# Folded products in 64-column halves, paired short pieces in the transforms, folds partly on VectorE, and all gates in the first stage: a gated mix of a spectral filter and a mixture of single-row experts

## The chip, the cores and the metric

The kernel runs on one core of a Trainium2 chip. The metric is the device time of one execution in microseconds (us). TensorE (PE, with its weight loads PEld), VectorE (DVE), ScalarE (ACT), GpSimd (POOL) and SyncE (SP) each run their own instructions in order; a queue issues its DMAs in order, and 16 DMA engines carry them.

## The reference

The input x has 2048 tokens of 576 numbers. One branch filters x in the spectrum, the other picks for each token and each of 32 heads one of 4096 experts by a product key (the best of 64 keys on the first half of a query, the best of 64 on the second), and a gate mixes the two.

```python
X = rfft2(x); y_a = irfft2(X * (w_r + 1j * w_i), (S, D))       # S=2048, D=576
q = einsum("nd,dhc->nhc", x, w_q); q1, q2 = q[..., :128], q[..., 128:]
s1 = einsum("nhd,ed->nhe", q1, k1); s2 = einsum("nhd,ed->nhe", q2, k2)
e = argmax(s1) * 64 + argmax(s2)                               # K = 1, so softmax is 1
y_b = einsum("nhk,nhkd->nd", gelu(einsum("nd,nhkd->nhk", x, u[e])), v[e])
g = sigmoid((x * gate_w).sum(-1)); out = g * y_a + (1 - g) * y_b
```

Rows of u and v lie side by side in memory, so that one gathered row is 4608 bytes. 2048 x 32 of them are 302 MB.

## The kernel before

The tokens make 16 tiles t of 128. The work has two stages that use the same memory after one another.

**Score stage.** Keys are folded into the query weights ahead of the scores: for each chunk c of four heads and each of five slices i of the model width, `build_m` multiplies the transposed query weights (tile `wq`, loaded by SP into the ring `uv`, L351) with the keys (`kT`): 8 matmuls of 128 columns each, of which 64 are used. ACT and one more pair of matmuls split the product into a high and a low part, `mh` and `ml`; there are 40 such builds. 64 steps (c, tp), one for each chunk and pair of tiles, then form the scores: 28 matmuls of 128x512 into one PSUM buffer `p`. DVE takes the maxima (`mx`, L463), ACT marks where the score equals its maximum (`sg`, L471, L482), DVE turns the marks of two steps into an index (`sq`, L488 to L499, `fe`, L502), and ACT writes it (`ei`, L504). Each tile's x is transposed on PE and split into `xh`, `xo`, `xq` (`split_x`).

From an index on, POOL gathers (L537; 512 gathers of 576 KB, four to a group) into the ring `uv` of 12 buffers, with 2 more (`uv2`) in the second stage. A group of one tile and one chunk is then: four dot products on DVE (L548), gelu on ACT (L554), weights on DVE (L561), and the sum over v either on DVE (L574) or by ACT (L586) and transposing matmuls on PE, with the total added from PSUM at L624 (`yt`). Tiles 0 to 9 (`E_T`) are gathered while scores are still formed, tiles 10 to 15 (`L_SEQ`, the late tiles) behind them.

**Transform stage.** When the memory of the score stage comes free, SP loads `kr` (L713), the late tiles' x (`xl`, L392), the matrix `fi` (L717), the gate's weights `gr` (L718), the filter `w` (L762) and twiddles `tw` (L755, then three copies on ACT, L756 to L758). 16 `fold`s multiply sums and differences of the two halves of a tile's columns with `kr`; ten units (`f2`, `f4`, `f5` on DVE at L781 to L784, `f6`) make the transform, the product with the filter and the way back; `invert` makes the output of each tile, and `mix` adds the branches. Between the folds and the units stand no barriers: gathers and sums of the late tiles go on beside them.

The order on each engine is set ahead by a planner (class `Plan`): a list scheduler that has a due time for each job (`when(s) = 16 + s * TPS` for step s, offsets `AT_*`, `AHEAD`, `TLAG`), a duration for each operation, delays between engines (`HOPS`) and for a gather (`LEAD`, `LAND`). Its result is the program; on the chip each engine follows it and waits where it must. It also decides which slot of a ring a buffer gets.

The gates: for tiles 0 to 9 the product x * gate_w and its sum are formed early (L399, with the weights in a `uv` buffer). For tiles 10 to 15 they are formed at the change of the stages (L403, `close_gates`) from `xl` and `gr`, followed by the sigmoid.

```python
plan("POOL", ISSUE, at - ahead, go, [(g, 0), (g, 1)], [("ei", t // 2, c)], move=MOVE, after=gate_by)
for n, t in enumerate(range(NT)):
    fold(t, T0 + AT_FOLD + FPACE * 1.3 * n)
```

## Time and profile before

| | us |
|---|---|
| runs, median of 3 | 963.69 (962.10 to 973.03) |
| profiled execution, its own time | 963.87 |
| its span | 962.1 |
| PE busy in the span | 912.2 (95%) |
| PEld / DVE / ACT / POOL busy | 770.5 / 827.3 / 649.7 / 576.5 |
| bytes moved by DMA | 344.17 MB, mean 358 GB/s |

The profile is one execution: a page of sums, and views that are asked of its trace. In a timeline row stand the start, the time from the first start to the last end, the engine, the line of the program, the operation with its output and inputs, the count, and in brackets the idle time before it and what ended it. A view of windows gives the busy time of each engine in stretches of the span, with the granted TensorE clock (PEclk) and the share of the DMA engines that was busy. A view of waits sums the idle time of an engine by what ended it. One fp32 matmul leaves two records of each kind, a PE record and a PEld record (the 640 records `p<-kT,uv` belong to the 320 matmuls of the 40 builds). A busy PE is not PE at its peak, since a matmul's end is modelled.

### The profile page before, as it was taken

Reading aid. Unit: us, or ns where it says so; the run is one execution under the profiler, and the core shown is the slowest. Engines: PE = TensorE matmul, PEld = TensorE weight load, DVE = VectorE, ACT = ScalarE, POOL = GpSimd, SP = SyncE. Lnnn points to the kernel's source line nnn. Section 1 sums busy time; section 2 is a strip of 40 time slices with the busy share of each in tenths; the row PEclk is TensorE's granted clock in tenths of the full one; section 3 lists DMA queues with packets and bytes.
Section 4 is the critical chain, followed back from the end, with each engine's and each line's share of the span. In section 5 each row is a group of like instructions: output and inputs, shape, how many; then the busy total and the mean of one; then the engine's idle time right before and its main releaser. Section 6 shows DMA issues by size and latency. Waiting matters only on the chain.

```text
span 962.1 us, 16497 instructions
## 1 busy us (share of the span) xinstructions
PE 912.2 (95%) x5192; PEld 770.5 (80%) x5192; DVE 827.3 (86%) x2019; ACT 649.7 (68%) x1970; POOL 576.5 (60%) x516
## 2 busy tenths in 40 slices
PE   7999999999999999999999996899999999999996
PEld 7888888878778878878778784678888888888875
DVE  1898889998999999998999997776788888868877
ACT  3697887787787788787788686344556566575444
POOL 0236546756756757757757666256766666677662
PEclk9999999999999999999999999899999999999999
DMA  9469969999999999999999999778999999999997
GB/s 340 155 242 339 386 255 358 387 357 359 367 356 339 396 343 372 383 347 366 374 350 339 355 368 406 296 284 328 409 410 410 409 409 406 408 404 413 413 415 254
DMA packets 89803, 344.17 MB, mean 358 GB/s; under 512 B 10098, under 2 KB 10612, under 8 KB 89716
## 3 DMA queue, kind: packets, MB, share of 16 engines
q0 software_dynamic: 73728, 302.02, 81.9%
q1 hardware_dynamic: 15988, 41.09, 11.3%
q8 instruction: 42, 0.69, 0.3%
q14 instruction: 45, 0.37, 0.1%
HBM read 338.35 MB, written 4.72 MB: 357 GB/s over the span
## 4 chain that ended last, share of the span: by engine, by line
PE 46%; DVE 24%; DMA 15%; ACT 7%; issue 6%; POOL 2%; DVEq 0%; SPq 0%; POOLq 0%; ACTq 0%
PE p L307 46%; DMA uv<-uv,ei 12%; DVE uv L548 8%; DVE xn L574 7%; ACT sg L471 3%; DVE mx L463 3%; ACT uv L586 3%; DMA gr<-gw 2%; POOL uv L537 2%; DVE sq L488 1%; DVE yt L624 1%; DMA kr<-t_kr 1%; DVE bt L848 0%; DVE sq L495 0%; DVE sq L496 0%
## 5 line engine op out<-in xcount | busy, mean ns | idle before, releaser
L537 POOL DMA_INDIRECT uv<-uv,ei x512 | 576.3, 1126 | 373.3 <-PE p L307 116.2
L471 ACT ACTIVATE sg<-p,mx 128x64 bf16<-128x64 f32 x1024 | 227.5, 361 | 53.0 <-DVE mx L463 46.0
L548 DVE SCALAR_TENSOR_TENSOR uv<-uv,xn 128x576 f32<-128x576 f32 x320 | 236.9, 753 | 19.3 <-DMA uv<-uv,ei 12.0
L307 PE MATMUL p<-mh,xh 128*128 128x512 f32 x512 | 204.3, 399 | 10.7 <-ACT sg L471 10.0
L574 DVE SCALAR_TENSOR_TENSOR xn<-uv,a,xn 128x576 f32<-128x576 f32 x248 | 201.7, 815 | 1.2
L586 ACT ACTIVATE uv<-uv,a 128x576 f32<-128x576 f32 x256 | 178.2, 768 | 35.0 <-DVE a L561 32.9
L307 PE MATMUL p<-ml,xh 128*128 128x512 f32 x512 | 200.5, 392 | 0.0
L307 PE MATMUL p<-mh,xo 128*128 128x512 f32 x512 | 200.2, 391 | 0.0
L548 DVE SCALAR_TENSOR_TENSOR uv<-uv,xl 128x576 f32<-128x576 f32 x192 | 142.1, 756 | 34.0 <-DMA uv<-uv,ei 32.8
L307 PE MATMUL p<-ident,uv 128*128 128x128 f32 x1310 | 161.5, 275 | 10.0 <-ACT uv L586 9.9
L307 PEld LDWEIGHTS p<-ident,uv 128*128 128x128 f32 x1310 | 144.9, 141 | 27.2 <-ACT uv L586 16.8
L307 PEld LDWEIGHTS p<-mh,xh 128*128 128x128 f32 x512 | 96.5, 188 | 29.6 <-ACT sg L471 11.2
L307 PEld LDWEIGHTS p<-mh,xo 128*128 128x128 f32 x512 | 96.5, 188 | 20.7
L307 PEld LDWEIGHTS p<-ml,xh 128*128 128x128 f32 x512 | 96.7, 189 | 17.4
L554 ACT ACTIVATE b<-z 128x4 f32<-128x4 f32 (+1 forms) x131 | 27.5, 210 | 113.4 <-DVE uv L548 112.6
L307 PE MATMUL p<-fi,bt 128*128 128x289 f32 x384 | 99.3, 410 | 0.1
L307 PEld LDWEIGHTS p<-fi,bt 128*128 128x128 f32 x384 | 83.1, 243 | 10.6 <-PE p L307 0.6
L463 DVE TENSOR_REDUCE mx<-p 128x16 f32<-128x1024 f32 x64 | 78.1, 1220 | 9.2 <-PE p L307 9.2
L307 PEld LDWEIGHTS p<-kT,uv 128*128 128x128 f32 x640 | 76.4, 194 | 2.5 <-PE p L307 0.5
L307 PE MATMUL p<-kT,uv 128*128 128x128 f32 x640 | 77.8, 277 | 0.4 <-PE p L307 0.3
L482 ACT ACTIVATE sg<-sg 128x256 bf16<-128x256 bf16 x192 | 71.8, 442 | 0.9
L307 PE MATMUL p<-mh,xq 128*128 128x512 f32 x128 | 50.1, 392 | 0.0
(107 smaller groups left out, 936.7 us busy)
## 6 DMA issues: line engine op xcount, KB each, us to landing
uv<-wqT SPq DMA_DIRECT2D x40, 512.0 KB, 6.7
uv<-uv,ei POOLq DMA_INDIRECT x512, 7.4
w<-wri SPq DMA_DIRECT2D x16, 289.0 KB, 6.7
out<-xn SPq DMA_DIRECT2D x13, 288.0 KB, 6.4
xn<-xn SPq DMA_DIRECT2D x10, 288.0 KB, 6.9
tw<-t_tw SPq DMA_DIRECT2D x9, 256.0 KB, 6.3
uv<-xn SPq DMA_DIRECT2D x6, 288.0 KB, 7.2
xl<-xn SPq DMA_DIRECT2D x6, 288.0 KB, 12.6
```

What stands on the lines that cost most here:

```text
L307: after("PE", nc.tensor.matmul(*args, **kw))
L463: dv(dve(1024), at, lambda: nc.vector.tensor_reduce(mv.ap[:, 2 * tp : 2 * tp + 2, :], ps.ap.rearrange("p a (g e) -> p a g e", e=E), AX.X, ...
L471: on("ACT", actv(sg.ap[:, j, g, :], ps.ap[:, j, g * E : g * E + E], AF.Sign, bias=mv.ap[:, 2 * tp + j, g : g + 1], scale=-1.0))
L482: ac(0.307, at, lambda b=b: actv(s2()[:, :, b * Q : b * Q + Q], s2()[:, :, b * Q : b * Q + Q], AF.Copy, bias=b / 4), [sg], [])
L488: dv(0.336, at, lambda: vt(sq.ap[:, k], s2()[:, :, : E // 2], s2()[:, :, E // 2 :], ALU.min), [(sq, k)], [sg])
L537: on("POOL", nc.gpsimd.indirect_dma_start(out=g.ap.rearrange("p a d -> p (a d)"), out_offset=None, in_=uv, in_offset=bass.IndirectOffsetOn ...
L548: dv(0.677, at, lambda k=k, g=rows[k]: stt(g.ap[:, 0, :], g.ap[:, 0, :], 1.0, x.ap, op0=ALU.mult, op1=ALU.mult, accum_out=z.ap[:, k : k + 1]),
L554: ac(0.1, at + AT_GELU, lambda k0=k0, k1=k1: actv(b.ap[:, k0:k1], z.ap[:, k0:k1], AF.Gelu_apprx_tanh), [(b, k0)], [(z, k) for k in ks], ta ...
L574: dv(0.731, at, lambda v=v, s=s: stt(y.ap, v(), s(), y.ap, op0=ALU.mult, op1=ALU.add), [y], [(rows[k], 1), (a, k)])
L586: ac(0.667, at + AT_SCALE, lambda k=k, v=v: actv(v(), v(), AF.Copy, scale=a.ap[:, k : k + 1]), [(rows[k], 1)], [(a, k)])
L624: dv(dve(n), at, lambda: vt(to(), of(), to(), ALU.add), [y], [pd])
```

## The change

Nothing of the mathematics changes. Six things do.

- `build_m`: 16 matmuls of 64 weight columns by 64 moving columns take the place of 8 of 128 by 128. They alternate between the upper and lower 64 output partitions; no unused column is formed.
- `fold`: for the 12 tiles of `FOLD_V`, DVE forms the sum and the difference of the two halves (two operations of 128x288), ACT copies 32 columns, and 6 matmuls follow: 4 of 128 columns and 2 of 64. For the other 4 tiles the same 12 matmuls stay, with equal widths next to each other.
- `f2` and `invert`: the third piece of a sum, two matmuls over 128 rows half of which met zeros, becomes two matmuls over 64 rows each (`tails`), next to each other. `f2` takes the two members of a pair in one go.
- All 16 gates are formed in the first stage, from x as `split_x` loaded it, late tiles first; `gr`, its load and the six products of L403 are gone. The sigmoid follows at once.
- The fifth transpose of `split_x` is 128 wide, as the others are.
- The planner: other delays, loads timed apart from gathers, a pace of 8.37 in place of 8.45, other due times (`AHEAD`, `TLAG`, `AT_*`), other steps for the builds, other pairs of late tiles. Lines of the program shift by about 10 (L351 becomes L357, L471 L482, L537 L548 and so on).

```diff
-                if got.move:
-                    dma = max(dma, t + (LEAD if eng == "POOL" else 1.96)) + got.move
-                    got.end = dma + (LAND if eng == "POOL" else 1.1)
+                if got.move and eng == "POOL":
+                    dma = max(dma, t + LEAD) + got.move
+                    got.end = dma + LAND
+                elif got.move:
+                    a = max(loads, t + 1.96)
+                    loads = a + got.move * (SLOW if dma > a else 1.0)
+                    dma = max(dma, a) + got.move
...
-            w = P if i < ND - 1 else D - 4 * P
-            mm(flat[:w, i * P : i * P + P], v[:, i * P : i * P + w], ident, is_transpose=True, skip_group_check=True, start=True, stop=True)
+            lo = min(i * P, D - P)
+            mm(flat[:, i * P : i * P + P], v[:, lo : lo + P], ident, is_transpose=True, skip_group_check=True, start=True, stop=True)
...
-    def gates(t, w, at, junk=None):
-        x = xs[t]
+    natural = {}
+
+    def gates(t, w, at):
+        x, v = natural[t]
         two = lambda a: a.rearrange("p (r d) -> p r d", r=2)
-        if junk is None:
-            out_ = lambda: two(w.ap[:, 1, :])
-            dv(dve(576), at, lambda: stt(
-                out_(), two(x.ap), 1.0, two(w.ap[:, 0, :]), op0=ALU.mult, op1=ALU.mult, accum_out=gz[:, t : t + 1]),
-                [("gz", t), (w, 1)], [x, (w, 0)])
-        else:
-            dv(dve(576), at, lambda: stt(
-                junk.ap[:, :, :288], two(x.ap), 1.0, two(w.ap), op0=ALU.mult, op1=ALU.mult, accum_out=gz[:, t : t + 1]),
-                [("gz", t), junk], [x, w])
+        dv(dve(576), at, lambda: stt(
+            two(w.ap[:, 1, :]), two(v()), 1.0, two(w.ap[:, 0, :]), op0=ALU.mult, op1=ALU.mult, accum_out=gz[:, t : t + 1]),
+            [("gz", t), (w, 1)], [x, (w, 0)])
+
+    def close_gates(at):
+        allz = [("gz", t) for t in range(NT)]
+        ac(0.2, at, lambda: actv(ge, gz, AF.Exp, scale=-1.0), ["ge"], allz, table="exp")
+        dv(0.1, at, lambda: nc.vector.tensor_scalar(ge, ge, 1.0, None, op0=ALU.add), ["ge"], [])
+        dv(0.2, at, lambda: nc.vector.reciprocal(gate, ge), ["gate"], ["ge"])
+        dv(0.1, at, lambda: nc.vector.tensor_scalar(gone, gate, -1.0, 1.0, op0=ALU.mult, op1=ALU.add), ["gone"], ["gate"])
+        dv(0.1, at, lambda: nc.vector.tensor_scalar(gsc, gate, 2.0 / (S * D), None, op0=ALU.mult), ["gsc"], ["gate"])
...
-                half = g % 2
-                mm(
-                    pv()[:, g, :], wq.ap[:, g, :],
-                    kTb.ap[:, half * 64 : half * 64 + 128], start=g % 4 == 0, stop=True, skip_group_check=True)
-
-        plan("PE", 8 * BUILT, at, go, [pm], [wq, kTb], after=after)
+                k = kTb.ap[:, g % 2 * E : g % 2 * E + E]
+                for m in (0, E):
+                    mm(pv()[m : m + E, g, :E], wq.ap[:, g, m : m + E], k, start=g % 4 == 0, stop=True, skip_group_check=True)
+
+        plan("PE", 8 * BUILT + 0.2, at, go, [pm], [wq, kTb], after=after)
...
-    for t in E_T:
-        gates(t, gw1, when(0) + GATE * t)
+    for n, t in enumerate(L_SEQ + E_T):
+        gates(t, gw1, when(0) + GATE0 + GATE * n)
+    close_gates(when(0) + GATE0 + GATE * NT)
...
-    ld(0.5, T0 + 15, lambda: nc.sync.dma_start(gw2.ap, gw.partition_broadcast(P)), [gw2])
...
+        if t in FOLD_V:
+            eo = buf("f5", [P, 640])
+            o, e, r = (eo, 0), (eo, 1), (eo, 2)
+            dv(dve(288), at, lambda: vt(eo.ap[:, 288:576], x.ap[:, :288], x.ap[:, 288:], ALU.add), [e], [x])
+            ac(0.12, at, lambda: actv(eo.ap[:, 576:608], x.ap[:, 288:320], AF.Copy), [r], [x])
+            dv(dve(288), at, lambda: vt(eo.ap[:, :288], x.ap[:, :288], x.ap[:, 288:], ALU.subtract), [o], [x])
+
+            def go():
+                pf = pb.ap.rearrange("p a b -> p (a b)")
+                for i, m0, lo, w in ((0, 0, 288, P), (1, 0, 416, P), (3, 0, 0, P), (4, 0, P, P), (2, 0, 544, E), (2, E, 256, E)):
+                    mm(pf[m0 : m0 + w, i * P : (i + 1) * P], eo.ap[:, lo : lo + w], kr.ap[:, 0, :], start=i in (0, 4), stop=True, skip_group_check=True)
+
+            plan("PE", 1.3, at, go, [pb], [o, e, r, (kr, 0)])
+            evacuate(t, pb, at)
+            return
 
         def go():
             pf = pb.ap.rearrange("p a b -> p (a b)")
-            for i, m0, lo, w, n, sign in ((0, 0, 0, P, P, 0), (1, 0, P, P, P, 0), (2, 0, 2 * P, E, 32, 0), (2, E, 2 * P, E, 32, 1), (3, 0, 0, P, P, 1), (4, 0, P, P, P, 1)):
-                for k, (at_, m) in enumerate(((lo, w), (DF - 1 + lo, n))):
-                    mm(pf[m0 : m0 + m, i * P : (i + 1) * P], x.ap[:, at_ : at_ + m], kr.ap[:, sign * k, :],
-                       start=i in (0, 4) and not k, stop=k == 1, skip_group_check=True)
-
-        plan("PE", 12 * 0.213, at, go, [pb], [x, (kr, 0), (kr, 1)])
+            hi = DF - 1
+            for i, m0, w, at_, sign, first, last in (
+                    (0, 0, P, 0, 0, 1, 0), (0, 0, P, hi, 0, 0, 1), (1, 0, P, P, 0, 0, 0), (1, 0, P, hi + P, 0, 0, 1),
+                    (3, 0, P, 0, 0, 0, 0), (3, 0, P, hi, 1, 0, 1), (4, 0, P, P, 0, 1, 0), (4, 0, P, hi + P, 1, 0, 1),
+                    (2, 0, E, 2 * P, 0, 0, 0), (2, E, E, 2 * P, 0, 0, 0), (2, 0, 32, hi + 2 * P, 0, 0, 1), (2, E, 32, hi + 2 * P, 1, 0, 1)):
+                mm(pf[m0 : m0 + w, i * P : (i + 1) * P], x.ap[:, at_ : at_ + w], kr.ap[:, sign, :],
+                   start=bool(first), stop=bool(last), skip_group_check=True)
+
+        plan("PE", 2.5, at, go, [pb], [x, (kr, 0), (kr, 1)])
+        evacuate(t, pb, at)
...
+    def tails(parts):
+        for o, b in parts:
+            for r in range(2):
+                for i in (3 * r, 3 * r + 1):
+                    mm(o(r), b(i), fi.ap[:, i, :], start=i == 3 * r, stop=False)
+        for o, b in parts:
+            for r in range(2):
+                mm(o(r), b(2)[r * E : r * E + E], fi.ap[r * E : r * E + E, 2 + 3 * r, :], start=False, stop=True)
+
+    def f2(qs, at):
+        ps = [psum() for _ in qs]
 
         def go():
-            for r in range(2):
-                for n, i in enumerate(((0, 1, 2), (3, 4, 2))[r]):
-                    mm(p.ap[:, r, :DF], BT.ap[:, i, :, q], fi.ap[:, 3 * r + n, :], start=n == 0, stop=n == 2)
-
-        plan("PE", 6 * pe(DF), at, go, [p], [fi, (fi, "ends"), (BT, "q", q)] + [(BT, "in", t, i) for t in range(NT) for i in range(2)])
-        return p
+            tails([(lambda r, p=p: p.ap[:, r, :DF], lambda i, q=q: BT.ap[:, i, :, q]) for p, q in zip(ps, qs)])
+
+        plan("PE", 5 * len(qs) * pe(DF) + 0.2, at, go, ps, [fi, (fi, "ends")] + [(BT, "q", q) for q in qs] + [(BT, "in", t, i) for t in range(NT) for i in range(2)])
+        return ps
...
+        pair = f2((k2,) if k2 in (0, 8) else (k2, 8 + k2), at)
+        pc = pair[0]
...
-    def close_gates(at):
-        jg = psum()
-        for t in L_SEQ:
-            gates(t, gw2, at, jg)
...
-            for r in range(2):
-                for m, i in enumerate((3 * r, 3 * r + 1, 2)):
-                    mm(p.ap[:, r, :DF], BT.ap[:, i, t * 8 : t * 8 + 8, :].rearrange("p j q -> p (j q)"),
-                       fi.ap[:, 3 * r + m, :], start=m == 0, stop=m == 2)
-
-        plan("PE", 6 * pe(DF), at, go, [p], [fi, (fi, "ends")] + every)
+            tails([(lambda r: p.ap[:, r, :DF], lambda i: BT.ap[:, i, t * 8 : t * 8 + 8, :].rearrange("p j q -> p (j q)"))])
+
+        plan("PE", 5 * pe(DF) + 0.2, at, go, [p], [fi, (fi, "ends")] + every)
...
-TPS = 8.45
-AHEAD = 15.44
-TLAG = 18.97
+TPS = 8.37
+AHEAD = 16.25
+TLAG = 18.2
 FPACE = 1.27
-BUILD = (1, 2, 5, 8, 8)
+BUILD = (2, 2, 4, 8, 8)
-_PAIRS = ((13, 14), (11, 10), (12, 15))
+_PAIRS = ((11, 14), (12, 10), (13, 15))
...
-GATE = 4.49
-HOLD_ML = 0.19
-HOLD_A = 0.14
+MOVE = 1.36
+X_GAP = 0.5
+GATE = 3.77
-AT_FOLD = -11.05
+AT_GELU = -7.79
+AT_SCALE = -15.89
+AT_SUM = -13.02
+AT_FOLD = -12.89
+FOLD_V = (1, 2, 3, 6, 7, 8, 9, 10, 11, 13, 14, 15)
+GATE0 = 7.52
```

Three places show how the order moves. The first is SP's queue behind the last load of query weights, with the semaphores that each load waits for. Before:

```order
L351 DMA uv_5700<-wqT 128x1024 [waits DMASW7_49,DMAHW3_49,DMASW5_49,DMAHW5_49,DMASW1_49,DVE_49]
L713 DMA kr_6640<-t_kr 128x128 [waits PE_49,Activation_49]
L392 DMA xl_6644<-xn 128x576
L392 DMA xl_6648<-xn 128x576
L392 DMA xl_6650<-xn 128x576 [waits DMAHW7_49]
L392 DMA xl_6652<-xn 128x576 [waits DMAHW0_49]
L392 DMA xl_6654<-xn 128x576 [waits DMAHW1_49]
L392 DMA xl_6657<-xn 128x576 [waits DMAHW2_49]
L717 DMA fi_6659<-t_fi 128x1734 [waits DMAHW3_49,PE_49,Activation_49]
L718 DMA gr_6661<-gw 128x576 [waits DMAHW4_49]
L762 DMA w_6663<-wri 128x578 [waits DMAHW5_49]
L755 DMA tw_6665<-t_tw 128x512 [waits DMAHW6_49]
```

After the change the same place reads:

```order
L357 DMA uv_5943<-wqT 128x1024 [waits DMASW5_49,DMASW3_49,DMAHW3_49,DMASW0_49,DMAHW6_49,PE_49,Activation_49]
L724 DMA kr_6937<-t_kr 128x128 [waits PE_49]
L400 DMA xl_6941<-xn 128x576 [waits PE_49]
L400 DMA xl_6945<-xn 128x576 [waits PE_49]
L400 DMA xl_6948<-xn 128x576 [waits DMAHW7_49,PE_49]
L400 DMA xl_6950<-xn 128x576 [waits DMAHW0_49]
L400 DMA xl_6952<-xn 128x576 [waits DMAHW1_49]
L400 DMA xl_6954<-xn 128x576 [waits DMAHW2_49]
L728 DMA fi_6956<-t_fi 128x1734 [waits DMAHW3_49,PE_49]
L800 DMA w_6958<-wri 128x578 [waits DMAHW4_49,PE_49]
L793 DMA tw_6962<-t_tw 128x512 [waits DMAHW5_49]
```

`gr` is gone, and the order is otherwise the same, but what the loads wait for is not: they lie over other buffers of the score stage. By the counts of the semaphores in the two programs, `kr` waited before for the 16th matmul from the end of the last step (63), and all behind it in the queue with it. Now `kr` waits for the end of step 55, the first `xl` loads for matmuls of step 56, `fi` for step 59, and only `w` and what follows it for step 63.

The second place is ACT's queue at the end of the scores, where the marks of the last step are made (`sg`). Before:

```order
L736 ACTIVATE bt_6755<-p_1104_6772 128x4x128
L471 ACTIVATE sg_6796<-p_1043_6562,mx_6068 128x64 x4
L737 ACTIVATE bt_6755<-p_1104_6772 128x128
L756 ACTIVATE tw_6665<-tw_6665 128x128
L471 ACTIVATE sg_6796<-p_1043_6562,mx_6068 128x64 x4
L757 ACTIVATE tw_6665<-tw_6665 128x2x128
L482 ACTIVATE sg_6796<-sg_6796 128x16x16
L758 ACTIVATE tw_6665<-tw_6665 128x128
L756 ACTIVATE tw_6669<-tw_6669 128x128
L482 ACTIVATE sg_6796<-sg_6796 128x16x16
L757 ACTIVATE tw_6669<-tw_6669 128x2x128
```

After:

```order
L482 ACTIVATE sg_7018<-p_1025_6753,mx_6424 128x64 x4
L767 ACTIVATE bt_7048<-p_1108_7026 128x4x128
L493 ACTIVATE sg_7018<-sg_7018 128x16x16
L768 ACTIVATE bt_7048<-p_1108_7026 128x128
L493 ACTIVATE sg_7018<-sg_7018 128x16x16 x2
L794 ACTIVATE tw_6962<-tw_6962 128x128
L795 ACTIVATE tw_6962<-tw_6962 128x2x128
L515 ACTIVATE ei_77<-fe_7092 128x4x4
L767 ACTIVATE bt_7048<-p_1109_7064 128x4x128
L768 ACTIVATE bt_7048<-p_1109_7064 128x128
L796 ACTIVATE tw_6962<-tw_6962 128x128
L794 ACTIVATE tw_6968<-tw_6968 128x128
```

Before, the copies of the first two twiddles (`tw`) stood between the marks of the last step, ahead of its index. Now they stand ahead of all marks of the last step (`sg_7178`, which begin some ten rows behind the last of them), around the index `ei_77` of the step pair before the last one. The rows `bt` are what the folds leave.

The third place is POOL's queue, where the first gathers of late tiles stand; `ei_75` to `ei_78` hold the indices of tiles 0 to 3, 4 to 7, 8 to 11 and 12 to 15. Before:

```order
L537 DMA uv_6896<-uv,ei_76 128x1152
L537 DMA uv_6964<-uv,ei_76 128x1152
L537 DMA uv_6968<-uv,ei_76 128x1152
L537 DMA uv_6990<-uv,ei_78 128x1152
L537 DMA uv_7008<-uv,ei_78 128x1152
L537 DMA uv_7030<-uv,ei_78 128x1152
L537 DMA uv_7050<-uv,ei_78 128x1152
L537 DMA uv_7069<-uv,ei_77 128x1152
```

After:

```order
L548 DMA uv_7307<-uv,ei_76 128x1152
L548 DMA uv_7320<-uv,ei_76 128x1152
L548 DMA uv_7327<-uv,ei_77 128x1152
L548 DMA uv_7340<-uv,ei_77 128x1152
L548 DMA uv_7383<-uv,ei_77 128x1152
L548 DMA uv_7396<-uv,ei_77 128x1152
L548 DMA uv_7415<-uv,ei_77 128x1152
L548 DMA uv_7429<-uv,ei_77 128x1152
L548 DMA uv_7446<-uv,ei_77 128x1152
L548 DMA uv_7452<-uv,ei_77 128x1152
L548 DMA uv_7463<-uv,ei_78 128x1152
L548 DMA uv_7470<-uv,ei_78 128x1152
```

Before, four gathers of tile 13, whose indices (`ei_78`) are last written behind step 63, stood behind the last that need `ei_76`, and ahead of gathers that need `ei_77`. Now eight gathers that need `ei_77`, last written behind step 61, stand ahead of the first that needs `ei_78`.

37 lines of the change are left out of this document (14 added, 23 removed).

## The prediction

> **What bounds the kernel now.** I read the page first, then four stretches of busy time, then the waits of PE and DVE in each, and last single rows at the change of the stages. The stretches show two kernels in one. Columns: stretch, length, then busy time of PE, PEld, DVE, ACT, POOL, the granted clock, the share of the DMA engines, the rate.
>
> ```profile
> 60.00:580.00 520.00, 501.59 (x2695) 425.00 (x2693) 493.42 (x1186) 405.91 (x1414) 336.04 (x287) 1.00 0.95 357
> 580.00:660.00 80.00, 68.06 (x475) 52.91 (x475) 56.38 (x144) 42.03 (x115) 37.16 (x36) 0.96 0.84 317
> 660.00:943.00 283.00, 278.53 (x1645) 237.41 (x1643) 229.55 (x578) 159.01 (x311) 190.26 (x179) 1.00 1.02 407
> 943.00:962.00 19.00, 10.71 (x66) 8.32 (x64) 14.26 (x31) 7.39 (x17) 4.07 (x4) 0.88 0.64 228
> ```
>
> In 60 to 580 us, the score stage, PE (96%), DVE (95%) and DMA (0.95) are all nearly full. From 660 on DMA is the limit (1.02, 407 GB/s). Between, nothing is full: PE 85%, DVE 70%, DMA 0.84. That hole of 80 us is where time lies open. The waits say who paces the score stage; first PE's, then DVE's, for 60 to 580 us.
>
> ```profile
> PE p L307 <- ACT sg L471: 10.0, 5, 2.0
> PE p L307 <- ACT uv L586: 5.8, 8, 1.0
> ...
> DVE uv L548 <- DMA uv<-uv,ei: 10.3, 15, 2.0
> DVE mx L463 <- PE p L307: 6.0, 8, 1.9
> DVE uv L548 <- PE p L307: 5.8, 5, 1.5
> ```
>
> PE and DVE take turns. DVE waits some 25 us in all, 11.8 of them (6.0 + 5.8) for PE, and 10.3 for gathers. So a faster PE can give about 12 us there, until DVE and the gathers stop it.
>
> **Step A, the builds in the score stage.** The row of one build before, its group, and one call of `f2` with moving pieces of 289 columns:
>
> ```profile
> 62.76 1.95 PE L307 MATMUL p<-kT,uv 128*128 128x128 f32 x16
> L307 PE MATMUL p<-kT,uv 128*128 128x128 f32 x640 | 77.8, 277 | 0.4 <-PE p L307 0.3
> 655.08 3.19 PE L307 MATMUL p<-fi,bt 128*128 128x289 f32 x12
> ```
>
> The 16 records of a build start every (1.95 - 0.277) / 15 = 0.112 us, so it costs 16 x 0.112 = 1.79 us. Those of 289 columns start every 0.25 us: the cost of a record goes with its moving columns (0.112 x 289 / 128 = 0.253). After, it has 32 records, each with half the weight columns and half the moving columns. Nothing here has that shape. The nearest row is the narrow part of `f6`, where weights of 33 columns alternate between two halves of the output partitions: nine records, 128 moving columns each, eight of them narrow.
>
> ```profile
> 675.93:676.40 0.47, 0.47 (x9) 1.00 0.95 382
> 675.93 0.37 PEld L307 LDWEIGHTS p<-tw,t 128*33 128x33 f32 x8 [0.33 <-issue]
> ```
>
> 0.47 / 8 = 59 ns, half of 112: the two halves overlap. With 64 moving columns a record costs between 59 ns (no gain from fewer columns: 32 x 0.059 = 1.88 us, nothing won) and half of it (0.94 us). By the proportion above I take the lower end, 0.9 us, and 0.2 us for the two changes of shape, by these gaps between full and narrow weights:
>
> ```profile
> 584.47 0.14 PEld L307 LDWEIGHTS p<-kr,xn 128*32 128x32 f32 x2 [0.17 <-issue]
> 584.80 0.19 PEld L307 LDWEIGHTS p<-kr,xn 128*64 128x64 f32 x2 [0.20 <-issue]
> ```
>
> 1.1 in place of 1.79 is 0.69 less, over the 35 builds behind the first chunk 24 us of PE work. Were there no overlap at all, 32 records of 112 ns would cost 3.6 us, 1.8 more than now.
>
> What DVE makes of it: 11.8 us of waits for PE go. Against that DVE gets six gate products more before 60 us. The early products and their accumulator reads take
>
> ```profile
> L399 DVE SCALAR_TENSOR_TENSOR uv<-xn,uv 128x576 f32<-128x576 f32 x10 | 7.5, 754 | 6.3 <-DMA uv<-gw 6.2
> L399 DVE DVE_READ_ACCUMULATOR uv<-xn,uv 128x1 f32 x10 | 0.8, 82 | 0.0
> 20.00:60.00 40.00, 38.41 (x213) 32.76 (x212) 31.57 (x77) 27.36 (x101) 8.78 (x9) 1.00 0.48 175
> ```
>
> 0.8 us apiece, 4.8 for six. DVE has 8.4 us free in 20 to 60, which hides part of them, but the fifth gather now stands behind the last gate in its ring buffer, so I charge all 4.8. The first stage then gains 11.8 - 4.8 = **7 us**. Bounds: below, 59 ns per record make a build 2.1 us, 0.29 more than now, 10 us over 35; of these PE's own 18 us of waits can take up some 8, so with the gates it is -7 (and worse where the halves don't overlap, rival 3). Above, 20 when DVE's waits all go: DMA, at 0.95, has 26 us left of 520, and 2.7 MB of loads (below) take 7 of them, so 19 to 20 is the most.
>
> A rule speaks against this step. The Trainium skill, Trainium Kernel Development and Optimization, section Performance Expectations, says that busy time of matmuls is a bad metric and that of the weight loads a good one. By that rule PEld's 425 of 520 us would leave PE 95 us of slack, and step A would be worth 0 and the sum 952, inside the forecast's own range. The rows speak against it: PE waits only some 18 us for anything in these 520, so I keep the 7.
>
> **Step B, the change of the stages.** The last score matmul starts at 579.63 us. 186 gathers are left at 654.37, and from there to the end DMA is full. What holds the work in between, from SP, DVE, ACT, POOL and PE (the row of L504 counts the last three indices and gives their first and last start):
>
> ```profile
> 579.63 0.39 PE L307 MATMUL p<-ml,xq 128*128 128x512 f32 x1
> 576.47 0.33 SPq L713 DMA_DIRECT2D kr<-t_kr  x1
> 576.85 2.81 SPq L392 DMA_DIRECT2D xl<-xn  x6
> 587.34 0.33 SPq L755 DMA_DIRECT2D tw<-t_tw  x1
> ...
> 602.51 0.77 DVE L403 SCALAR_TENSOR_TENSOR p<-xl,gr 128x576 f32<-128x576 f32 x1 [6.53 <-DMA gr<-gw]
> 606.65 0.31 ACT L756 ACTIVATE tw<-tw 128x128 f32<-128x128 f32 x1 [7.82 <-DMA tw<-t_tw]
> 610.91 0.31 ACT L756 ACTIVATE tw<-tw 128x128 f32<-128x128 f32 x1 [2.33 <-DMA tw<-t_tw]
> 612.17 0.43 DVE L488 TENSOR_TENSOR sq<-sg 128x512 bf16<-128x512 bf16 x1 [3.78 <-ACT sg L482]
> 619.71 1.21 POOL L537 DMA_INDIRECT uv<-uv,ei  x1 [13.03 <-DVE xn L574]
> 604.80 25.80 PE L307 MATMUL p<-kr,xn 128*128 128x128 f32 x168 [7.65 <-DVE yt L624]
> 631.92 1.26 POOL L537 DMA_INDIRECT uv<-uv,ei  x1 [6.92 <-PE p L307]
> 654.37 0.94 POOL L537 DMA_INDIRECT uv<-uv,ei  x1 [5.50 <-PE p L307]
> L504 ACT ACTIVATE ei<-fe x3: 217/263/333, 575.4 to 617.8; 128x16 uint32<-128x16 f32 x3
> 654.00:962.00 308.00, 198.74 (x186) 0.99 0.99 392
> ```
>
> Read downward: `kr`, six `xl`, `fi`, `gr` are issued at once at 576 us beside gathers, so `gr` is late (DVE idles 6.53 us) and `tw` behind it is later (ACT idles 7.82 and 2.33 with the last marks behind it, which DVE then misses for 3.78). The index of the last step comes at 617.8, and POOL, whose next gathers need it, stands 13.03 us; the releaser named had been done for long. Then one block of folds, 25.8 us on PE, keeps transposing sums from freeing buffers: 6.92 and 5.50.
>
> After the change: the gate products and `gr` are gone from here; `kr`, `xl` and `fi` wait for steps 55 to 59 and not for step 63, and land before the scores end, so `tw` is third in the queue behind `w`; POOL has eight gathers of `ei_77` to issue while `ei_78` is being made. And a fold on VectorE costs PE 8 x 0.112 + 4 x 0.059 + 0.2 = 1.3 us; before it was
>
> ```profile
> 591.97 3.54 PE L307 MATMUL p<-kr,xn 128*128 128x128 f32 x24
> ```
>
> 24 records for one fold, 3.3 us apart. 12 x 2.0 us, and some 0.7 for each of the other four, take about 27 us from PE. On DVE they add 24 sums of half a tile, by the row of that size
>
> ```profile
> L784 DVE TENSOR_TENSOR t<-t,t 128x289 f32<-128x289 f32 x16 | 7.3, 458 | 0.0
> 580.00:654.00 74.00, 62.06 (x436) 47.02 (x436) 54.86 (x139) 37.74 (x108) 32.75 (x31) 0.95 0.86 326
> 576.00:600.00 24.00, 16.86 (x110) 12.79 (x108) 19.88 (x49) 16.30 (x58) 14.54 (x15) 1.00 1.03 406
> ```
>
> 24 x 0.458 = 11.0 us, and take away six gates, 4.8. DVE then needs 54.9 + 11.0 - 4.8 = 61 us of the 74 that the stretch 580 to 654 takes now. DMA moves 24.1 MB there (74 us at 326 GB/s); at the 406 GB/s of 576 to 600 that is 59 us, and without the 3.0 MB that went ahead or away 52. So DVE sets the floor, 61 us, and the gain lies between 0 (the folds' sums fill the gaps that the waits leave) and 13 if DVE never waits; 22 if folds on DVE slip behind 654 and only DMA's floor counts. In the rows above POOL stands 13.03 + 6.92 + 5.50 = 25 us, each time for something that the change brings earlier; but DVE's waits for gelu stay,
>
> ```profile
> DVE a L561 <- ACT b L554: 10.2, 6, 3.4
> ```
>
> so I count half of it: **12**, near DVE's floor.
>
> On the loads moved ahead the same page of the Trainium skill, section Key Constraints, says that DMAs of all queues run on the same 16 engines and interleave. By that rule the 2.7 MB would cost their 7 us in the score stage if DMA were full there, and the sum would be 952; the trace's share of 0.95 leaves room for them, so the sum stays.
>
> **Step C, units and inverts.** In each `f2` and `invert` (16 and 16 calls) 12 records of 289 columns become 8 full ones and 4 over 64 rows. By the row of `f2` in step A a record takes 0.25. If two halves overlap, a call saves 0.5 us: 16 us, less the change of shape there and back at 25 places for 0.17, is 12 us of PE. If rows don't overlap, it loses 4. But in 660 to 943 DMA is at 1.02 with 407 GB/s: the 186 gathers left at 654.4 need their time whatever PE does. **0 us**, and 4 either way at most. The tail behind the last gather keeps its operations: 0.
>
> **Sum.** 963.9 (the profiled execution's own time, 0.2 above the median of the runs) - 7 - 12 - 0 = **945**.
>
> **The rivals.**
> 1. *Both holes close fully.* The score stage gains 20 (DVE never waits, DMA full) and the stages' change 22 (DMA's floor): 922. For it: PE, DVE and DMA all get slack or earlier work. Against it: DVE had 95% already, and its waits for gathers (10.3) don't go by a faster PE. Between this and the forecast lie 930 to 937 as well.
> 2. *Narrow records don't get cheaper.* 59 ns is a floor. The first stage then loses 10 - 8 + 4.8 = 7 us, the change of the stages gains its 12: 959, no change that can be told. For it: 59 ns is the shortest pitch in the rows above. Against it: those records had 128 moving columns.
> 3. *The halves don't overlap in the builds* (slower). 40 builds of 32 records make 1.28 us of PE for each ns of a record. By the sums above (35 times what a build costs over 1.79, less 8, plus 4.8, less 12) the change pays nothing at 63 ns and is 1% slower from 72 ns on. At 80 ns a build is 2.76 us: 35 x 0.97 - 8 + 4.8 - 12 = +19, 983. For it: no row shows 64-wide weights alternating. Against it: 33-wide ones did overlap.
>
> **Chances.** The forecast's own case, 938 to 954: 0.53. Rival 1: 0.22. Rival 2: 0.15. Rival 3: 0.10. A measurement of this kernel tells 1% from no change, so within 1% is 954.2 to 973.5: rival 2. Leaving out rival 3 and the lower half of rival 1's stretch (0.1 of its chance) the range is 922 to 961. Faster by over 1%: 0.75; within: 0.15; slower: 0.10.
>
> **What would show it.** A build as 32 records in about 1.1 us (near 2.1: rival 2; over 2.5: rival 3). DVE's waits for PE in the score stage near 0, the last score matmul near 572. `kr` and `xl` issued long before the scores end, no idle of ACT for `tw` and none of POOL over 5 us, the 326th gather some 19 us earlier, about 635; from there to the end the same 308 us. I am wrong if gathers, held up by the loads moved ahead, become DVE's wait in the score stage, or if the time from the 326th gather to the end changes.

## The result and the profile after

The changed kernel takes 957.55 us (median of 20 runs, 951.57 to 964.05) against 967.42 for the kernel before (20 runs, 962.10 to 973.03): 0.9905 of the time, 95% interval 0.9881 to 0.9928. It is faster, by 9.9 us, where 19 were forecast. 957.55 lies in the range, which reaches down into the second rival's stretch; the gain is half of the forecast's and within the 1% that was given a chance of 0.15. One part of the distance is the starting point: the profile of before (963.87) and the median that was shown (963.69) lie among the fastest of its 20 runs.

The profiled execution of the changed kernel is one of its longest (963.8 us, span 961.9). A second profile of the same kernel, from the experiments below (956.98 us, span 955.2), stands nearer to the median. The stretches of both, in the columns shown for before:

```profile
60.00:580.00 520.00, 490.64 (x3198) 403.84 (x3199) 487.64 (x1175) 404.18 (x1405) 321.75 (x283) 0.98 0.96 357
580.00:660.00 80.00, 66.18 (x419) 53.25 (x419) 75.83 (x187) 51.64 (x157) 53.70 (x48) 0.89 0.95 358
660.00:943.00 283.00, 267.17 (x1586) 216.53 (x1586) 221.63 (x562) 155.44 (x305) 185.55 (x175) 0.98 1.01 400
```

```profile
60.00:580.00 520.00, 492.22 (x3220) 404.93 (x3220) 491.23 (x1187) 408.44 (x1419) 325.64 (x285) 0.98 0.96 360
580.00:660.00 80.00, 61.80 (x406) 49.11 (x406) 76.87 (x188) 48.48 (x148) 55.24 (x49) 0.91 0.97 374
660.00:943.00 283.00, 268.84 (x1595) 218.28 (x1595) 221.41 (x563) 155.04 (x303) 186.48 (x173) 0.98 1.01 398
```

The hole at 580 to 660 is closed: in the second profile DVE is busy for 96% of it (70% before), and DMA has 0.97 (0.84). The score stage moves no more bytes per second than before (357 and 360 GB/s), though PE is less busy. And behind 660 the rate has fallen from 407 GB/s to 398 to 400, which the prediction had as fixed. PE's granted clock is down in every stretch (0.98, 0.89 to 0.91, 0.98; before 1.00, 0.96, 1.00).

Measured by marks in the traces (us). "First chunk" is from the first maximum of chunk 0 to that of chunk 1, "a later chunk" the mean of the next six, then the start of the last score matmul, from there to the start of the 326th gather (counted from 0: 186 are left with it), and from that gather to the end:

| profile | first chunk | a later chunk | last score matmul | to 326th gather | to the end |
|---|---|---|---|---|---|
| before | 75.1 | 72.0 | 579.6 | 74.7 | 307.7 |
| changed, the long run | 81.8 | 72.2 | 582.6 | 64.3 | 315.0 |
| changed, the second profile | 81.8 | 71.6 | 578.3 | 62.6 | 314.4 |

So by these marks the score stage gained nothing that both profiles show, the change of the stages gained 10 to 12 us, and the rest lost 7. How the last two share it hangs on the mark. In the kernel before, the gather ahead of it starts as below, and then POOL stands 5.50 us:

```profile
647.40 1.47 POOL L537 DMA_INDIRECT uv<-uv,ei  x1 [0.31 <-DVE a L561]
```

Counted from this gather, the change of the stages takes 67.8 us before and 62.2 and 60.5 in the two profiles of the changed kernel, and the time from it to the end 314.7, 317.1 and 316.4. Then the change of the stages gained 6 to 7 us, and the rest lost 2. The sum is the same, its parts are known to some 5 us.

The loads in the second profile, from SP's timeline, then the view of the index's line (the last four, with their first and last start), then POOL's timeline:

```profile
519.14 0.33 SPq L724 DMA_DIRECT2D kr<-t_kr  x1
523.90 5.03 SPq L400 DMA_DIRECT2D xl<-xn  x6
549.04 0.33 SPq L728 DMA_DIRECT2D fi<-t_fi  x1
575.48 0.42 SPq L793 DMA_DIRECT2D tw<-t_tw  x1
```

```profile
L515 ACT ACTIVATE ei<-fe x4: 215/216/232, 562.2 to 613.0; 128x16 uint32<-128x16 f32 x4
```

```profile
607.24 1.21 POOL L548 DMA_INDIRECT uv<-uv,ei  x1 [6.03 <-DVE xn L585]
...
623.10 1.03 POOL L548 DMA_INDIRECT uv<-uv,ei  x1 [3.29 <-PE p L313]
...
640.86 1.07 POOL L548 DMA_INDIRECT uv<-uv,ei  x1 [0.97 <-ACT t L863]
```

`kr`, `xl` and `fi` go out 31 to 57 us earlier than before, and where POOL stood 13.03, 6.92 and 5.50 us it stands 6.03, 3.29 and 0.97. One of 5.32 us at 563.2 us is new; before, the longest between 555 and 600 us was 3.04.

### The profile page after: what moved, and what is told of

It is laid out like the page before. It is cut to its first block, busy times and chain, and to the rows that moved or that the text cites. A ratio compares the mean times of both kernels' runs of the same rounds, so it can differ in the third digit from the quotient of the medians.

```text
span 961.9 us, 17535 instructions
## 1 busy us (share of the span) xinstructions
PE 883.3 (92%) x5688; PEld 723.0 (75%) x5688; DVE 833.4 (87%) x2043; ACT 651.1 (68%) x1980; POOL 571.5 (59%) x516
## 4 chain that ended last, share of the span: by engine, by line
PE 37%; DVE 31%; DMA 18%; ACT 10%; issue 3%; POOL 1%; SPq 0%; ACTq 0%; DVEq 0%; POOLq 0%
PE p L313 37%; DMA uv<-uv,ei 15%; DVE uv L559 10%; DVE xn L585 8%; DVE mx L474 4%; ACT sg L482 4%; DMA tw<-t_tw 3%; ACT uv L597 2%; DVE yt L635 1%; DVE sq L499 1%; POOL uv L548 1%; DVE sq L507 1%; ACT L565 1%; DVE im L510 1%; DVE a L572 0%
## 5 line engine op out<-in xcount | busy, mean ns | idle before, releaser
L548 POOL DMA_INDIRECT uv<-uv,ei x512 | 571.3, 1116 | 375.2 <-PE p L313 73.0
L482 ACT ACTIVATE sg<-p,mx 128x64 bf16<-128x64 f32 x1024 | 231.4, 360 | 45.8 <-DVE mx L474 42.3
L313 PE MATMUL p<-mh,xh 128*128 128x512 f32 x512 | 209.8, 410 | 20.8 <-ACT sg L482 14.3
L313 PE MATMUL p<-ml,xh 128*128 128x512 f32 x512 | 204.7, 400 | 0.0
L313 PE MATMUL p<-mh,xo 128*128 128x512 f32 x512 | 204.3, 399 | 0.0
L313 PE MATMUL p<-ident,uv 128*128 128x128 f32 x1310 | 168.2, 282 | 21.4 <-ACT uv L597 20.4
L313 PEld LDWEIGHTS p<-ident,uv 128*128 128x128 f32 x1310 | 150.0, 145 | 42.6 <-ACT uv L597 26.9
L313 PE MATMUL p<-fi,bt 128*128 128x289 f32 (+1 forms) x384 | 90.5, 432 | 1.1 <-ACT bt L767 0.7
L313 PEld LDWEIGHTS p<-fi,bt 128*128 128x128 f32 (+1 forms) x384 | 68.2, 242 | 18.9 <-issue 9.8
L313 PE MATMUL p<-ml,xq 128*128 128x512 f32 x128 | 50.1, 391 | 0.0
L313 PEld LDWEIGHTS p<-kT,uv 128*64 128x64 f32 x1280 | 41.0, 142 | 9.2 <-issue 4.3
```

The costliest lines, as they stand in the source:

```text
L313: after("PE", nc.tensor.matmul(*args, **kw))
L482: on("ACT", actv(sg.ap[:, j, g, :], ps.ap[:, j, g * E : g * E + E], AF.Sign, bias=mv.ap[:, 2 * tp + j, g : g + 1], scale=-1.0))
L548: on("POOL", nc.gpsimd.indirect_dma_start(out=g.ap.rearrange("p a d -> p (a d)"), out_offset=None, in_=uv, in_offset=bass.IndirectOffsetOn ...
```

## The experiments

Each kernel was timed in turns with the kernel before on the same chip. Unless said otherwise every engine's order is that of the kernel which was edited.

**The narrow builds alone, in the kernel before.**

```diff
-    mm(pv()[:, g, :], wq.ap[:, g, :], kTb.ap[:, half * 64 : half * 64 + 128], ...)
+    for m in (0, E):
+        mm(pv()[m : m + E, g, :E], wq.ap[:, g, m : m + E], k, ...)
```

> The kernel before with one edit: the folded products as 16 narrow matmuls a build, every engine's order as before. The prediction (PE sets part of the score stage's pace): 7 to 12 us faster, 955 to 960 where before is 967, and DVE's waits for PE near 0. Theory D (DVE and the gathers set the pace, what PE saves turns into idle): the eight chunks keep their 72.5 us each, the time stays within 3 us of before. Theory C (idle lowers PE's granted clock, and that costs what the builds saved): more than before's three cold stretches, and a time equal to before or up to 5 us longer.

963.59 us against 966.73: ratio 0.9966 (0.9948 to 0.9984), 3 us. A build is as cheap as forecast: in the changed kernel (the long run) two of them, 64 records, take

```profile
112.50 2.08 PE L313 MATMUL p<-kT,uv 128*64 128x64 f32 x64
```

and the records of one build start every 30.0 ns, the lower end that the prediction took. Yet of 24 us less work on PE, 3 arrive. A later chunk takes 71.5 us in place of 72.0. PE's waits, then DVE's, in 60 to 580 us of this run:

```profile
PE p L307 <- ACT uv L585: 13.4, 9, 2.4
PE p L307 <- ACT sg L470: 13.0, 6, 2.5
PE p L307 <- ACT mh L421: 4.2, 5, 1.7
```

```profile
DVE uv L547 <- DMA uv<-uv,ei: 9.2, 16, 1.9
DVE mx L462 <- PE p L307: 5.9, 8, 1.8
DVE uv L547 <- PE p L307: 4.7, 6, 1.3
```

PE's waits for ACT's marks and scaled rows grew from 15.8 to 26.4 us; DVE's waits for PE stayed (10.6 for 11.8). PE's busy time in these 520 us fell from 501.6 to 484.9 us, by 16.7, and all its waits for ACT grew from 17.4 to 30.6. So most of what the builds save PE spends standing for ACT, and DVE waits for PE nearly as long as before.

**The wide builds back in the changed kernel.** The same edit the other way.

```diff
-    for m in (0, E):
-        mm(pv()[m : m + E, g, :E], wq.ap[:, g, m : m + E], k, ...)
+    mm(pv()[:, g, :], wq.ap[:, g, :], kTb.ap[:, half * 64 : half * 64 + 128], ...)
```

> The changed kernel with one edit: the folded products again as 8 wide matmuls a build (1.79 us in place of 0.95), every engine's order as after the change. The prediction: 7 to 24 us longer than the changed kernel's 957. Theory D: chunks keep their 72.5 us, the time stays within 3 us. Theory C: the seven cold stretches of the score stage fall to three or fewer, and the time is 945 to 955, shorter than after the change.

956.94 us, as the changed kernel (957.55). In the new order the narrow builds are worth nothing that can be told. The stretches of a cold PE clock in the score stage (told below) fell from seven in the long run and five in the second profile to two, and that was worth nothing either: behind the first chunk neither PE's work nor its clock sets the pace alone.

**The late tiles' gate products cut.**

```diff
-    two(w.ap[:, 1, :]), two(v()), 1.0, two(w.ap[:, 0, :]), ...
+    two(w.ap[:, 1, :n]), two(v()[:, :n]), 1.0, two(w.ap[:, 0, :n]), ...   # n = 4 for tiles 10 to 15
```

> The changed kernel with the six early gate products of the late tiles cut to 4 of 576 columns (the late tiles' gates leave the rest of the sum out), order unchanged. Theory D: these products cost DVE time in the first chunk, which took 81.8 us against 75.1 before; it shortens by 3 to 4 us, and the whole with it, 953 to 955. If the first chunk is long for another reason (PE's cold clock at 27 to 35 us, the new places of loads and builds): less than 1 us.

956.15 us; the first chunk took 78.9 us where the changed kernel's two profiles have 81.8. Profiles of other kernels with the same early order lie at 79.5 to 82.1, so the six products cost 1 to 3 us of the first chunk's 6.7; the total shows 1.4, too little for four runs to settle. What the rest of the first chunk's loss comes from was not tried alone. The traces show where most of it lies: from the first to the third maximum 22.2 us pass before (24.71 to 46.91) and 26.8 in the second profile (22.87 to 49.67), and there PE's granted clock is 0.50 for 6.83 us from 27.7 on, where before it is 1.00.

**DVE's and DMA's part of the pace.** One kernel takes 27 us from DVE in the score stage, one adds 26 us of DMA.

```diff
-    g.ap[:, 0, :], g.ap[:, 0, :], 1.0, x.ap, ...
+    g.ap[:, 0, :496], g.ap[:, 0, :496], 1.0, x.ap[:, :496], ...    # tiles 0 to 9
```

> Again the changed kernel with the early tiles' dot products over 496 of 576 columns (80 are left out), 27 us less of DVE's work in the score stage. Theory D: 15 to 25 us shorter than the changed kernel beside it, a chunk 2 to 3 us shorter. If the gathers and their round trip set the pace: within 4 us of it.

949.30 us against 957.37 for the changed kernel beside it: 8 us. A later chunk takes 70.1 us, and the last score matmul starts 10 us earlier.

```diff
+    nc.sync.dma_start(w.ap[:, :4], wqT[c, i][:, :4])
     nc.sync.dma_start(w.ap, wqT[c, i])
```

> Again the changed kernel with half of the query weights loaded twice, 10.5 MB or 26 us of DMA more in the score stage. DVE's 27 us less shortened the whole by 8 us, so DVE is part of what sets the pace. If DMA sets the rest: 15 us or more longer than the changed kernel. If the rest is the wait of each engine on the next in a fixed order, with DMA's slack left: 2 to 8 us longer.

972.72 us (1.0039 of before, 1.0004 to 1.0074), 15 us more than the changed kernel's other runs; the last score matmul starts at 594.8. DVE's waits for gathers, in 60 to 580 us, of the changed kernel's long run, of the short dots and of the added bytes:

```profile
DVE uv L559 <- DMA uv<-uv,ei: 15.1, 19, 3.1
```

```profile
DVE uv L560 <- DMA uv<-uv,ei: 20.4, 27, 3.2
```

```profile
DVE uv L564 <- DMA uv<-uv,ei: 18.1, 24, 3.4
```

The added bytes have a second effect. Each stands in SP's queue right ahead of the load that a build needs, and in the same stretch PE waits for query weights, which it never does in the second profile:

```profile
PE p L313 <- DMA uv<-wqT: 15.7, 9, 3.0
```

So the 15 us may be the price of late weights as well as of a busy DMA; this run doesn't part the two. Of a microsecond of work in the score stage 0.3 arrives if it is DVE's (removed), 0.1 or nothing if it is PE's (removed or put back), and at most 0.6 if it is DMA's (added). None of the three edits returns its full price, so no engine alone is shown to set the pace. That the gathers and DVE share it fits the rows; the ring of 12 buffers was not changed in any run.

**The folds back on PE.**

```diff
-    dv(...eo[288:576], x[:288] + x[288:]); ac(...eo[576:608]); dv(...eo[:288], x[:288] - x[288:])   # and 6 matmuls
+    12 matmuls on x.ap for all 16 tiles; no sums, no copies
```

> Again the changed kernel with all folds as 12 matmuls on PE and no sums on DVE, order unchanged. If the folds on VectorE carry the stages' change: the 326th gather 70 us or more behind the last score matmul in place of 64, and 5 to 9 us longer than the changed kernel beside it. If not: within 2 us of it.

960.12 us, 2.8 more than the changed kernel beside it; from the last score matmul to the 326th gather 66.6 us in place of 62.6. The stretch 580 to 660:

```profile
580.00:660.00 80.00, 74.11 (x563) 61.32 (x562) 66.21 (x162) 49.80 (x146) 52.07 (x46) 0.98 0.94 351
```

PE has 12 us more to do there, DVE 11 less. Between the two expectations: by the two profiles the folds on VectorE carry 4 of this stretch's 12 us (one gather earlier 1.5 of 7.3). The 2.8 us of the total are not clear of noise, with four runs of each.

**The early loads held back.**

```diff
-    ld(0.2, T0 - 20, ... kr ...)                                  # the same for xl and fi
+    ld(0.2, T0 - 20, ... kr ..., held=score_jobs[7, 5][:1])       # xl: steps 61, 62; fi: step 63
```

> Again the changed kernel with kr, xl and fi held back to steps 61 to 63, order unchanged (the last time the memory was slower in all runs of the call). If these loads carry the stages' change: the 326th gather 67 us or more behind the last score matmul in place of 63 to 64, 960 or more. If they cost the score stage: its last chunk shorter by 1 to 2 us and 953 to 956. If neither: 956 to 959.

962.75 us, 5 more than the changed kernel's other runs (five runs, 957.4 to 967.2; their ratio to before, 0.9918, 0.9886 to 0.9950, is not clear of the changed kernel's), and 67.9 us to the 326th gather in place of 62.6 to 64.3: the early loads carry 4 to 5 us of the 10 to 12, by one profile, the longest of the five. Held back they don't make the score stage shorter: its later chunks take 72.0 us, and the last one, from its first to its last maximum, 64.3 in place of 60.9. The rest, some 3 us, is left for the missing gate products and the gathers of `ei_77`, which were not tried alone; counted one gather earlier almost nothing is left for them.

**The full pieces back in the transforms.**

```diff
-    mm(o(r), b(2)[r * E : r * E + E], fi.ap[r * E : r * E + E, 2 + 3 * r, :], start=False, stop=True)
+    mm(o(r), b(i), fi.ap[:, 3 * r + n, :], start=n == 0, stop=n == 2)      # three pieces of 128 rows each
```

> The changed kernel with the short pieces of the transforms again as two matmuls over 128 rows with zeros, order unchanged. It gives PE back some 12 us of work behind 660 us. The prediction (DMA is the limit there): the same time as the changed kernel within 2 us. Theory C: fewer cold stretches behind 660 us than the four of the changed kernel, and a time up to 5 us shorter. If PE sets the pace there: 8 to 12 us longer.

961.58 us (0.9949 of before, 0.9930 to 0.9968), 4 us longer than the changed kernel. In the new order PE's work in the transforms counts, for about a third of the 12 us.

**The new operations in the old order**: narrow builds, and the short pieces side by side within each `f2` and `invert`.

> The kernel before with two of the new operations, the narrow builds and the short pieces side by side, in the old order. The narrow builds alone gave 3 us. The prediction (DMA limits the transforms): nothing more, 963 to 965, and 308 us from the 326th gather to the end. Theory P there (PE's work counts): 4 us more, as undoing the short pieces cost in the new order, 958 to 961.

963.58 us, the same as with the narrow builds alone; 307.3 us from the 326th gather to the end. In the old order the short pieces are worth nothing that can be told, as predicted: DMA stays at 407 GB/s from 660 to 900 us. These two operations bring 3 to 5 us (0.9956, 0.9931 to 0.9981); the rest of the gain comes with the folds, the gates and the new order.

**What slows the stretch behind the 326th gather.** First the due times of the late tiles' groups as before:

```diff
-    at + AT_GELU, at + AT_SCALE, at + AT_SUM, AHEAD, TLAG
+    at - 5.94, at - 15.44, at - 15.91, 15.44, 18.97               # for tiles 10 to 15
```

> The changed kernel with the due times of the late tiles' groups as before the change (their gelu, scaling, sum, gathers and start; the score stage's order untouched). From the 326th gather to the end it took 312 to 317 us after the change and 308 before. Theory O (the new late order makes DVE and PE wait for ACT): 308 to 310 us there, and 4 to 6 us shorter than the changed kernel. If the operations (narrow pieces, cold PE) cost it: no change there.

957.41 us; 312.6 us to the end, 2 less than in the second profile, and no gain in the time. Theory O, which asked for 308 to 310, falls. The changed kernel itself beside it, whose profile is the second one above:

> The changed kernel itself, beside the variants of this call, since the last call's times of the kernel before were 18 us longer than in the others and held no changed kernel to compare with. All theories: about 9 us below the kernel before where that takes 967; above it, if the changed kernel bears a slower memory worse.

957.37 us, 0.9890 of before (0.9844 to 0.9935). ACT's rows in it told what is late:

```profile
658.54 0.31 ACT L794 ACTIVATE tw<-tw 128x128 f32<-128x128 f32 x1 [4.67 <-DMA tw<-t_tw]
686.40 0.31 ACT L794 ACTIVATE tw<-tw 128x128 f32<-128x128 f32 x1 [6.68 <-DMA tw<-t_tw]
711.80 0.31 ACT L794 ACTIVATE tw<-tw 128x128 f32<-128x128 f32 x1 [3.85 <-DMA tw<-t_tw]
```

ACT stands for twiddles at the head of its queue, in the second profile five times for 18.0 us behind 640 us; in the kernel before never behind 640 us. The planner now takes a load to run beside the gathers and not behind them, and so places ACT's copies earlier than the twiddles land. With loads behind step 63 timed as before:

```diff
+    elif got.move and t > self.queued_from:                       # T0 + 5
+        dma = max(dma, t + 1.96) + got.move
+        got.end = dma + 1.1
```

> The changed kernel with the planner timing loads behind step 63 as before the change, queued behind the gathers; the order up to there is unchanged, and behind it ACT's copies of the twiddles stand four to eight rows later. Theory W (ACT, in order, stands for twiddles that the planner expects too early, and gelus and scaled rows behind it wait): ACT's waits for tw fall from 17 to 27 us to under 8, the 326th gather to the end takes 308 to 310 us in place of 312 to 317, and the time is 3 to 6 us shorter than the changed kernel's 957. If DMA alone limits that stretch or PE's cold clock does: no change.

No wait for a twiddle is left behind 640 us. The stretch 660 to 900 us in the kernel before, in the second profile of the changed kernel, and here:

```profile
660.00:900.00 240.00, 235.53 (x1434) 202.75 (x1432) 196.77 (x502) 137.55 (x270) 163.52 (x154) 1.00 1.02 407
```

```profile
660.00:900.00 240.00, 228.24 (x1381) 188.05 (x1382) 188.04 (x484) 135.10 (x263) 159.60 (x149) 0.97 1.01 398
```

```profile
660.00:900.00 240.00, 228.51 (x1399) 185.45 (x1398) 194.05 (x494) 137.79 (x271) 161.56 (x152) 1.00 1.02 407
```

DMA is back at 407 GB/s, and the 326th gather to the end takes 310.3 us, 4 less (4 less also when counted one gather earlier). That the waits go and the rate comes back is shown, the gain of the whole is not: 957.18 us by four runs, where 3 to 6 us less were expected. Its score stage, unchanged in order, ended at 584.4 in the profiled run, 6 us later than in the second profile; why is open.

**Two groups of slower runs.** In two groups of runs every kernel took longer, the one before 985 and 983 us. The expectations call this a slower memory; the traces don't show that. The kernel with its early loads held back has a profile of each kind. Two of its waits over the whole span, in the run above and then in the slower group:

```profile
DVE uv L559 <- DMA uv<-uv,ei: 38.8, 57, 3.5
PE p L313 <- issue: 1.6, 1, 1.6
```

```profile
PE p L313 <- issue: 25.8, 40, 3.2
DVE uv L559 <- DMA uv<-uv,ei: 18.0, 25, 1.6
```

In the slower run DVE waits less for gathers, not more, and PE stands 25.8 us where the profile shows nothing that it waits for ("issue"); for DVE and ACT that sum goes from 1.4 and 2.8 us to 26.3 and 54.8. What slowed these runs stays open. They settle nothing of their own questions; the kernels of the first group, whose edits are those told above, ran again with the results given there.

> The changed kernel with all 16 folds as 12 matmuls on PE (2.5 us each) and without the 24 sums and 12 copies, every engine's order unchanged. The prediction counted the folds on VectorE as part of the 12 us of the stages' change. If they carry it: the 326th gather, 64 us behind the last score matmul after the change and 75 before, falls back to 70 or more and the time is 962 to 967. If the early loads, the missing gate products and the gathers of ei_77 carry it: 64 to 66 us, and 956 to 959.

1013.5 us.

> The changed kernel with its early loads held back: kr and the first xl for step 61 in place of 55 and 56, the other xl for step 62, fi for the middle of step 63 as before the change; order unchanged. If the early loads carry the stages' change: the 326th gather 68 us or more behind the last score matmul, time 960 to 965. If they cost the score stage time (DMA is nearly full there): the last chunk, 61 to 62 us from its first to its last maximum against 60.2 before, falls by 1 to 2 us and the time is 955 to 957. If neither: 956 to 959.

1004.1 us.

> The changed kernel with the 320 dot products of the early tiles over 496 of 576 columns (80 columns of u are left out there), order unchanged: 0.083 us less each, 27 us of DVE's work in the score stage. Theory D (DVE sets the pace): a chunk falls from 71.5 by 2 to 3 us, the whole by 15 to 25, to 932 to 942. If the gathers set it (DMA, or the round trip through the ring of 12 buffers): within 4 us of 957. Theory P (PE sets it) was met by 3 us for 24 us of PE's work in the kernel before.

1005.3 us.

> The changed kernel with half of each slice of query weights loaded twice: 10.5 MB more in the score stage, 26 us of DMA at 407 GB/s; order unchanged. If DMA sets the pace of the score stage: 15 to 26 us longer, 972 to 983. If DVE does: less than 5 us longer.

1012.6 us. All four are slower than the kernel before (1.0165 to 1.0241), among them the one with 27 us less of DVE's work.

**The late loads again, and a warm tail.** The second group held the late loads once more, by the edit above:

> Again the changed kernel with loads behind step 63 timed as before. The stretch from the 326th gather to the end was 310 us in place of 314, but four runs had the median of the changed kernel. If that gain is real: 952 to 955 by more runs, where the changed kernel has 957.5. If not: 957.

998.24 us against 982.53 (1.0146, 1.0081 to 1.0211). Whether this version is faster than the changed kernel stays open.

```diff
+    for i in range(14):
+        mm(w.ap[:, 0, :P], ident, ident, start=True, stop=True, ...)     # ahead of the last tile's last sums
```

> The same with 14 matmuls of the identity by itself, into a PSUM buffer that nobody reads, ahead of the last tile's last sums, where PE idles 4.1 us; all else as in the run beside it. Theory C for the tail (idle, then a cold clock on the path): the 20 transposing sums take 2.8 us in place of 4.5 and the five behind them 0.9 in place of 1.4, the stretch from the last gather to the end 14 us in place of 16, and the whole 2 us shorter. If the clock is not on the path: no change.

1000.98 us, no shorter than the run beside it. The last sums in the second profile of the changed kernel, and here:

```profile
944.72 3.73 PE L313 MATMUL p<-ident,uv 128*128 128x128 f32 x20 [4.12 <-ACT uv L597]
949.25 1.41 PE L313 MATMUL p<-ident,f 128*128 128x128 f32 x5 [0.79 <-ACT f L618]
```

```profile
989.56 3.29 PE L317 MATMUL p<-ident 128*128 128x128 f32 x28
993.85 2.77 PE L317 MATMUL p<-ident,uv 128*128 128x128 f32 x20 [1.00 <-ACT uv L601]
997.44 0.86 PE L317 MATMUL p<-ident,f 128*128 128x128 f32 x5 [0.83 <-ACT f L627]
```

The idle matmuls keep the clock up and the sums get 1.0 and 0.6 us shorter, but the stretch from the last gather to the end did not (15.5 us; 15.1 in the run beside it). The cold clock there is shown, a cost on the path is not. By one slower profile of each, this is a weak test.

## Why the prediction was off

**Step A failed: the term of 11.8 us.** The builds came out at the size that was taken (30 ns a record). What failed is "11.8 us of waits for PE go". The prediction read two rows, DVE waiting for PE, as time that a faster PE gives back. The narrow builds alone left those rows nearly as they were (10.6) and lengthened PE's own waits for ACT. In the changed kernel the waits for PE did shrink, to 8.8 us in the long run and 5.8 in the second profile, but DVE's waits as a whole did not: 31.1 and 27.3 us, 24.9 before. The two largest rows of the second profile:

```profile
DVE uv L559 <- DMA uv<-uv,ei: 14.2, 16, 2.4
DVE mx L474 <- PE p L313: 2.5, 2, 1.5
```

The row for gathers was 10.3 before. That it grows is a sign by which the prediction called itself wrong. The loads moved ahead are not the cause that it named for this: held back, they leave the row at 14.7. A row of waits names who came last at that moment, not who sets the cycle; in a loop of DVE, ACT, PE and a ring of gathers each is last now and then. The experiments measured the pace: 3 us for 24 of PE, 8 for 27 of DVE, and 15 for 26 of DMA, with late weights in it. In its place, by the second profile, the score stage began 1.8 us earlier, lost 6.7 in the first chunk, gained 2.4 in the next six and 3.8 in the last: 1.3 us in all, where 7 were forecast; in the long run it lost 3. The gates' 4.8 us were charged too high: the six products cost 1 to 3. That the first chunk lost more than 4.8 has mostly another reason. The rule that was weighed against this step (the Trainium skill, Trainium Kernel Development and Optimization, section Performance Expectations: busy time of matmuls misleads, that of the weight loads tells) stood nearer to the runs: by it PE had slack and the step was worth 0.

**Step B came out near its number.** 12 us were forecast from the last score matmul to the 326th gather, 10.4 and 12.2 are in the two profiles; the signs came too (early loads, shorter stalls of POOL), but for stalls of 6.03 and 5.32 us where none over 5 was to be left. Some of this is luck: half of POOL's 25 us was a judgement, and one gather earlier the gain is 6 to 7. DVE became the busy engine as forecast (77 of the 80 us from 580 to 660). The parts, by that mark: the early loads 4 to 5, the folds on VectorE 2 to 4 (at full clock a fold's 12 records take 1.4 to 1.5 us where 1.3 was forecast), the rest not told apart.

**Step C failed: 0 us "whatever PE does", with DMA full.** It holds in the old order, where the short pieces brought nothing. In the new order DMA is not always full behind 640 us: 398 GB/s from 660 to 900, where it was 407. ACT stands for twiddles; that what it holds up keeps buffers from POOL is argued, but with these waits gone the rate is 407 again. The twiddles cost, by one profile each, 4 us of the 6.6 that this stretch lost. PE's work counts there too (4 us for the short pieces), probably because engines then wait for each other. Another 2.2 us (2.9 in the long run) lie behind the last gather: 15.3 and 16.1 us to the end in place of 13.1, where the prediction had put 0 for the tail; what makes it longer stays open. The prediction had compared the order of ACT at one place only, around the last marks, and not the later copies of twiddles.

**The rivals.** The second came nearest in its number (959), by the wrong mechanism: narrow records did get cheaper. The first and third fell, the third with the pitch of 30 ns. What was missing is a rival in which the loads' new times in the planner put an engine's wait in a new place, and a chance higher than 0.15 that PE's savings don't arrive.

**The sum**, by the second profile: the score stage -1.3, the stages' change -12.2, the rest +6.6, together -6.9 against the profiled execution of before, where -19 was forecast. One gather earlier it reads -1.3, -7.3, +1.7.

## What to carry to other kernels

Before counting a wait as gain, ask who would be last next: a small experiment that takes work from one engine at a time tells the pace of a loop, the busy shares and the table of waits don't. Look at what else such an edit delays: the doubled loads held up the ones behind them. A mark beside a long stall moves time from one stage to the next, so try a second one. When a planner's model of loads changes, look at every in-order queue that consumes them: a copy placed a few rows too early holds up all that stands behind it. And a stretch that is "full of DMA" stays so only while no engine in the ring of buffers falls behind.
